# Layer scale on one core: the HBM layout in two blocks of 64 rows, and one head of 8 rows instead of two of 4

## The chip, the cores and the metric

The kernel runs on one core of one Trainium2 chip. The metric is device time in microseconds (us); the kernel before takes 119.68 us, the median of three runs (119.56 to 119.86). Of the core, this kernel uses VectorE (DVE) for the arithmetic, TensorE (PE) for one small product and to pass signals on, and the queues of SyncE (SP) and ScalarE (ACT) to issue transfers. The transfers of both queues are carried out by the same 16 DMA engines, in packets.

## The reference

```
B, S, D = 1024, 16, 512          # all bf16
def reference(x, y, gamma):      # x, y: [B, S, D]; gamma: [D]
    return x + gamma * y
```

Per call 16.78 MB of x and as much of y are read and 16.78 MB are written, 50.33 MB in all, for one multiplication and one addition per element.

## The kernel before, in words

The tensors are taken as 16384 rows of 512 elements (1 KB each), 128 rows to each of the 128 partitions of the on-chip memory (SBUF). The list BLOCKS (L7) cuts HBM into blocks: a block of n rows holds 128 n rows of the tensor, and partition p takes n that follow each other. So in the block of 64 rows each partition's data is one run of 64 KB, in that of 60 rows one of 60 KB, and in the first block one of 4 KB. A transfer of n rows then moves one packet of n KB for each partition, and each DMA engine serves 8 partitions.

All of y (128 KB per partition) has its place in y_sb, where the result also is formed. x_sb holds only 76 rows: the second part of x goes over rows of the first part that have been added. The fourth number of an x entry in the lists below is its row in x_sb.

The order of the work is written out by hand, in three lists:

- SP (L12 to L19): y 0 to 4, y 4 to 68, x 4 to 68, y 68 to 128, x 68 to 120, x 120 to 128.
- ACT (L20): x 0 to 4, gamma, then the stores 4 to 68, 0 to 4 and 68 to 128.
- DVE (L28): multiplications ("m") and additions ("a") over the PIECES of 8, 16, 44, 52 and 8 rows (L9). Multiplication is y_sb = y_sb * gamma_sb (L180), addition is y_sb = x_sb + y_sb (L189).

The function ring (L113) issues a list in its order. EARLY says how many of a list's first transfers are moved ahead of the program's opening barrier (L197 to L203). AHEAD says at which entry the queue waits for the signal s_held, which TensorE gives when the transfer HOLD, y 0 to 4, has landed (L147 to L149). So x 4 to 68 and what follows it on SP, and gamma on ACT, are issued only then. A load of x into rows of x_sb that were used waits for the additions of the pieces there (frees, L102). A store waits for the additions of its rows; the first store also waits for s_go, which TensorE gives when RELEASE, x 68 to 120, has landed (L157 to L159). DVE takes the same landing through s_rel.

gamma is one row; a product on TensorE with a column of ones spreads it over the partitions (L152) and DVE copies it to gamma_sb (L154). The multiplications need it. The program ends on SP's wait for all stores (L195).

Of the kernel before, what the change touches and what calls it, by code (L numbers as in the profile page):

```python
# [3 lines left out]

BLOCKS = [4, 64, 60]  # L7

PIECES = [8, 16, 44, 52, 8]  # L9


SP = [  # L12
    ('y', 0, 4),
    ('y', 4, 68),
    ('x', 4, 68, 4),
    ('y', 68, 128),
    ('x', 68, 120, 24),
    ('x', 120, 128, 0),
]  # L19
ACT = [('x', 0, 4, 0), ('g',), ('s', 4, 68), ('s', 0, 4), ('s', 68, 128)]  # L20

EARLY = (2, 1)

HOLD, AHEAD = ('y', 0, 4), (2, 1)

RELEASE = ('x', 68, 120, 24)

DVE = [('m', 0), ('m', 1), ('m', 2), ('a', 2), ('a', 0), ('a', 1), ('m', 3), ('m', 4), ('a', 3), ('a', 4)]  # L28
MULT, ADD = mybir.AluOpType.mult, mybir.AluOpType.add


def _take(sem, n, eng):


    return eng.wait_ge(sem, n).then_inc(sem, -n)  # L35


def kernel(
# [18 lines left out]
    rows = N // P  # L57
    n = len(PIECES)
    assert sum(PIECES) == rows
    starts = [sum(PIECES[:c]) for c in range(n + 1)]  # L60
    dt = xf.dtype
    edges = [sum(BLOCKS[:c]) for c in range(len(BLOCKS) + 1)]
    assert edges[-1] == rows

    def rows_of(t, a, b):

        c = max(c for c in range(len(BLOCKS)) if edges[c] <= a)
        assert b <= edges[c + 1]
# [6 lines left out]
    y_sb = nc.alloc_sbuf_tensor("y_sb", [P, rows, D], dt).ap()  # L75
    x_loads = [w for w in ACT + SP if w[0] == "x"]
    y_loads = [w for w in SP + ACT if w[0] == "y"]
    stores = [w for w in SP + ACT if w[0] == "s"]
    for loads in (x_loads, y_loads, stores):
# [9 lines left out]
    s_add, s_go, s_rel, s_end, s_out = sem("s_add"), sem("s_go"), sem("s_rel"), sem("s_end"), sem("s_out")  # L89
    added = [a for kind, *a in DVE if kind == "a"]  # L90
    order = {a[0]: k for k, a in enumerate(added)}

    def meets(a, b, c, d):
        return a < d and c < b
# [4 lines left out]
    def x_at(row):  # L99
        return next(w[3] + row - w[1] for w in x_loads if w[1] <= row < w[2])  # L100
# [12 lines left out]
    def ring(eng, what, n_early, n_ahead):  # L113

        known, went = 0, False
        for k, w in enumerate(what):
            kind = w[0]
            if k == n_ahead:
                _take(s_held[eng], 1, eng)
            need = frees(w) if kind == "x" else pieces_of(w[1], w[2]) + list(w[3:]) if kind == "s" else []  # L120
            need = max((order[c] + 1 for c in need), default=0)
            if kind == "s" and not went:
                _take(s_go, 1, eng)
                went = True
            if need > known:
                eng.wait_ge(s_add, need)
                known = need
            if kind == "g":
                i = eng.dma_start(out=gamma_row, in_=gamma.unsqueeze(0)).then_inc(s_gamma, 16)
            elif kind == "x":  # L130
                to = x_sb[:, w[3] : w[3] + w[2] - w[1], :]
                i = eng.dma_start(out=to, in_=rows_of(xf, w[1], w[2])).then_inc(s_load[w], 16)
            elif kind == "y":
                r = slice(w[1], w[2])
                i = eng.dma_start(out=y_sb[:, r, :], in_=rows_of(yf, w[1], w[2])).then_inc(s_load[w], 16)
            else:
                r = slice(w[1], w[2])
                i = eng.dma_start(out=rows_of(of, w[1], w[2]), in_=y_sb[:, r, :]).then_inc(s_out, 16)
            if k < n_early:
                early.append(i.ins)  # L140

    ring(nc.sync, SP, EARLY[0], AHEAD[0])
    ring(nc.scalar, ACT, EARLY[1], AHEAD[1])

# [11 lines left out]

    _take(s_load[RELEASE], 16, nc.tensor)  # L157
    nc.tensor.sem_inc(s_go, 1)
# [4 lines left out]
    def need(loads, c):  # L163
        for w in loads:
            if w not in landed and meets(starts[c], starts[c + 1], w[1], w[2]):
                if w == RELEASE:
                    _take(s_rel, 1, nc.vector)
                elif w == HOLD:
                    _take(s_held[nc.vector], 1, nc.vector)
                else:  # L170
                    _take(s_load[w], 16, nc.vector)
                landed.add(w)

    for kind, *args in DVE:
        c = args[0]
        yt = y_sb[:, starts[c] : starts[c + 1], :]
        if kind == "m":
            need(y_loads, c)
            g = gamma_sb[:, None, :].to_broadcast([P, PIECES[c], D])
            nc.vector.tensor_tensor(out=yt, in0=yt, in1=g, op=MULT).then_inc(s_dve, 1)  # L180
            open_mults += 1
        else:
# [4 lines left out]
            at = x_at(starts[c])  # L187
            xt = x_sb[:, at : at + PIECES[c], :]
            nc.vector.tensor_tensor(out=yt, in0=xt, in1=yt, op=ADD).then_inc(s_add, 1)  # L189
# [44 lines left out]
```

## Time and profile before

| What | us |
|---|---|
| Median of three runs | 119.68 (119.56 to 119.86) |
| Profiled execution: its span, which is the time that the profile gives for it | 118.2 |
| DVE busy | 70.1 (59% of the span) |
| PE busy | 0.6 |
| DMA, mean over the span | 426 GB/s |

The page of the profile lists busy time by engine, the DMA queues (q1 is SP's, q10 is ACT's) with the share of 16 engines' span that their packets took, and groups of instructions by line. The time of a DMA issue (SPq, ACTq) is only that of issuing; the transfer runs on after it. Windows cut the span at chosen moments and give, for each stretch, its duration, the busy time of the engine asked for with its number of instructions, the TensorE clock, the DMA engines' busy share and what they moved. A packet is counted where it starts, so the share of a short window can pass 1.

### The profile page before, as it was taken

How to read it: one execution, taken by the hardware profiler on the slowest of the kernel's cores; microseconds unless marked ns; L12 is line 12 of the kernel's file. 1: busy time of each engine (PE TensorE's matmuls, PEld its weight loads, DVE VectorE, ACT ScalarE, POOL GpSimd, SP SyncE). 2: the span in 40 equal slices, each digit the busy share in tenths (PEclk: the TensorE clock that was granted, in tenths of full speed). 3: DMA queues.
4: the chain of work that ended last, by engine and by line, in shares of the span. 5: the costliest groups of instructions: out<-in, count | busy, mean ns of one | idle time of the engine just before them, and what ended most of it. 6: DMA issues, size and time to landing. Idle time of an engine off the chain costs nothing. (4 is left out here: it accounts for less than half of the span.)

```text
span 118.2 us, 91 instructions
## 1 busy us (share of the span) xinstructions
PE 0.6 (0%) x1; PEld 0.1 (0%) x1; DVE 70.1 (59%) x12; POOL 0.2 (0%) x4
## 2 busy tenths in 40 slices
PE   0000100000000000000000000000000000000000
PEld 0000000000000000000000000000000000000000
DVE  0000200089999969999999999999999900000000
POOL 0000000000000000000000000000000000000000
DMA  6999889988899879879969696898899889799793
GB/s 248 461 666 399 355 355 399 665 355 355 355 599 466 355 333 624 374 333 499 499 288 576 288 576 288 360 637 355 355 576 488 355 355 510 333 582 416 333 499 166
DMA packets 1442, 50.33 MB, mean 426 GB/s; under 512 B 161, under 2 KB 162, under 8 KB 546
## 3 DMA queue, kind: packets, MB, share of 16 engines
q1 hardware_dynamic: 864, 33.03, 64.8%
q10 hardware_dynamic: 578, 17.30, 33.9%
HBM read 33.56 MB, written 16.78 MB: 426 GB/s over the span
## 5 line engine op out<-in xcount | busy, mean ns | idle before, releaser
L180 DVE TENSOR_TENSOR y_sb<-y_sb,gamma_sb 128x4096 bf16<-128x4096 bf16 (+3 forms) x5 | 34.7, 6981 | 10.9 <-DVEq L35 10.9
L189 DVE TENSOR_TENSOR y_sb<-x_sb,y_sb 128x4096 bf16<-128x4096 bf16 (+3 forms) x5 | 34.7, 6981 | 1.2 <-DVEq L35 1.1
L154 DVE CAST gamma_sb<-gamma_ps 128x512 bf16<-128x512 f32 x1 | 0.7, 692 | 10.2 <-DVEq L35 10.2
L146 DVE MEMSET ones_row<- 1x128 bf16 x1 | 0.2, 165 | 2.0 <-PEq L51 2.0
L152 PE MATMUL gamma_ps<-gamma_row,ones_row 1*128 1x512 bf16 x1 | 0.6, 581 | 11.6 <-PEq L35 11.6
L152 PEld LDWEIGHTS gamma_ps<-gamma_row,ones_row 1*128 1x128 bf16 x1 | 0.1, 101 | 11.6 <-issue 11.6
L218 POOL MEMSET const-bfloat16-1.0<- 128x1 bf16 x1 | 0.1, 101 | 0.0
L218 POOL MEMSET const-uint8-127<- 128x1 uint8 x1 | 0.1, 101 | 0.0
L218 POOL MEMSET const-float32-0.0<- 128x1 f32 x1 | 0.1, 98 | 0.2 <-issue 0.2
L218 POOL MEMSET const-float32-1.0<- 128x1 f32 x1 | 0.1, 98 | 0.0
## 6 DMA issues: line engine op xcount, KB each, us to landing
y_sb<-in_y_dram SPq DMA_DIRECT2D x1, 7680.0 KB, 57.3
out_dram<-y_sb ACTq DMA_DIRECT2D x1, 7680.0 KB, 23.8
x_sb<-in_x_dram SPq DMA_DIRECT2D x1, 6656.0 KB, 21.7
x_sb<-in_x_dram SPq DMA_DIRECT2D x1, 1024.0 KB, 22.0
y_sb<-in_y_dram SPq DMA_DIRECT2D x1, 512.0 KB, 3.4
x_sb<-in_x_dram ACTq DMA_DIRECT2D x1, 512.0 KB, 4.2
out_dram<-y_sb ACTq DMA_DIRECT2D x1, 512.0 KB, 22.3
y_sb<-in_y_dram SPq DMA_DIRECT2D x1, 23.4
```

Of the source, the lines that this page charges most:

```text
L146: nc.vector.memset(ones_row, 1.0).then_inc(s_ones, 1)
L152: nc.tensor.matmul(gamma_ps, ones_row, gamma_row, start=True, stop=True).then_inc(s_ps, 1)
L154: nc.vector.tensor_copy(out=gamma_sb, in_=gamma_ps).then_inc(s_dve, 1)
L180: nc.vector.tensor_tensor(out=yt, in0=yt, in1=g, op=MULT).then_inc(s_dve, 1)
L189: nc.vector.tensor_tensor(out=yt, in0=xt, in1=yt, op=ADD).then_inc(s_add, 1)
L218: nc = _bacc.Bacc("TRN2", target_bir_lowering=False, num_devices=1)
```

## The change

HBM is cut into two blocks of 64 rows, so each partition's data lies in two runs of 64 KB. The two heads of 4 rows (y on SP, x on ACT) become one head, the first 8 rows of y on SP; those are rows of the block, 8 KB for each partition out of its 64. Behind it SP loads y 8 to 64, x 0 to 64, y 64 to 128, x 64 to 120 and x 120 to 128. ACT has no load ahead of the barrier and issues gamma and two stores of 64 rows, where it had three stores. HOLD and RELEASE name the transfers that now stand in these places. The pieces are 20, 44, 56 and 8 rows, in eight DVE instructions instead of ten. x_sb keeps 76 rows (20 + 56).

```
-BLOCKS = [4, 64, 60]
-PIECES = [8, 16, 44, 52, 8]
+BLOCKS = [64, 64]
+PIECES = [20, 44, 56, 8]
 SP = [
-    ('y', 0, 4),
-    ('y', 4, 68),
-    ('x', 4, 68, 4),
-    ('y', 68, 128),
-    ('x', 68, 120, 24),
+    ('y', 0, 8),
+    ('y', 8, 64),
+    ('x', 0, 64, 0),
+    ('y', 64, 128),
+    ('x', 64, 120, 20),
     ('x', 120, 128, 0),
 ]
-ACT = [('x', 0, 4, 0), ('g',), ('s', 4, 68), ('s', 0, 4), ('s', 68, 128)]
-EARLY = (2, 1)
-HOLD, AHEAD = ('y', 0, 4), (2, 1)
-RELEASE = ('x', 68, 120, 24)
-DVE = [('m', 0), ('m', 1), ('m', 2), ('a', 2), ('a', 0), ('a', 1), ('m', 3), ('m', 4), ('a', 3), ('a', 4)]
+ACT = [('g',), ('s', 0, 64), ('s', 64, 128)]
+EARLY = (2, 0)
+HOLD, AHEAD = ('y', 0, 8), (2, 0)
+RELEASE = ('x', 64, 120, 20)
+DVE = [('m', 0), ('m', 1), ('a', 1), ('a', 0), ('m', 2), ('m', 3), ('a', 2), ('a', 3)]
```

## The prediction

> **What bounds the kernel now.** I read the page's head and its DMA parts first, then the windows cut where the packet size changes, then the timeline around the hand-overs, then the groups by shape.
>
> ```profile
> span 118.2 us, 91 instructions
> PE 0.6 (0%) x1; PEld 0.1 (0%) x1; DVE 70.1 (59%) x12; POOL 0.2 (0%) x4
> ...
> q1 hardware_dynamic: 864, 33.03, 64.8%
> q10 hardware_dynamic: 578, 17.30, 33.9%
> ```
>
> The two DMA queues together keep the 16 DMA engines busy for 64.8 + 33.9 = 98.7% of the span; VectorE (DVE) has 59%. The chain of waits ends in the second store as 12.53 us of "issue" between two adds, which tells nothing here: the bound is the DMA engines. The windows say how well each stretch of them runs (duration, DVE busy, clock, DMA share, GB/s):
>
> ```profile
> 1.00:3.65 2.65, 0.17 (x1) 1.00 0.98 385
> 3.65:42.36 38.71, 19.11 (x4) 1.00 1.01 434
> 42.36:60.51 18.15, 17.07 (x4) 1.00 1.00 433
> 60.51:76.26 15.75, 15.75 (x3) 1.00 1.00 433
> 76.26:78.75 2.49, 2.34 (x2) 1.00 1.09 464
> 78.70:98.03 19.33, 15.69 (x2) 1.00 1.01 437
> 98.03:99.28 1.25, 0.00 (x0) 1.00 0.92 377
> 99.28:117.80 18.52, 0.00 (x0) 1.00 0.99 428
> ```
>
> In order these are: both 4-row heads (4 KB packets); y and x of rows 4 to 68 (64 KB packets); y 68 to 128 (60 KB); x 68 to 120 (52 KB); x 120 to 128 (8 KB); store 4 to 68; store 0 to 4 (4 KB); store 68 to 128. A packet is counted at its start, so a window's edge can borrow bytes: the fifth window's 464 holds first packets of the store, and by its own bytes x 120 to 128 is 1.049 MB / 2.49 us = 421 GB/s. No stretch after 3.65 waits for anything: each begins where the last ends, at 433 to 434 GB/s. All that can be won lies in the head (385) and the short store (377); all that can be lost is a hole between two transfers. How near the holes are, the timeline shows:
>
> ```profile
> 0.00 0.85 SPq L135 DMA_DIRECT2D y_sb<-in_y_dram  x2
> 0.13 0.38 ACTq L132 DMA_DIRECT2D x_sb<-in_x_dram  x1
> ...
> 3.90 0.50 ACTq L129 DMA_DIRECT2D gamma_row<-in_gamma_dram  x1
> ...
> 12.32 0.69 DVE L154 CAST gamma_sb<-gamma_ps 128x512 bf16<-128x512 f32 x1 [10.16 <-DVEq L35]
> ...
> 55.37 2.53 SPq L132 DMA_DIRECT2D x_sb<-in_x_dram  x2
> 61.80 16.22 DVE L180 TENSOR_TENSOR y_sb<-y_sb,gamma_sb 128x26624 bf16<-128x26624 bf16 x2
> 77.41 17.36 ACTq L138 DMA_DIRECT2D out_dram<-y_sb  x3
> 78.17 16.23 DVE L189 TENSOR_TENSOR y_sb<-x_sb,y_sb 128x26624 bf16<-128x26624 bf16 x2
> ```
>
> The first packet comes 1.00 us after the first issue. The last adds end at 78.17 + 16.23 = 94.40, the second large store is issued at 94.43 (the page's last DMA row has 23.8 us from there to landing, which is the span's end), and its packets begin at 99.28 only because the queue is full until then: 4.9 us to spare.
>
> **The change part by part.** The bytes stay 50.33 MB, so I sum stretches of DMA time from 1.00 on.
>
> *Head.* Two 4-row transfers on two queues (8 + 8 packets of 4 KB per engine) become one of 8 rows on SP's queue (8 packets of 8 KB per engine), the same 1.049 MB; ACT loses its early issue. Nearest rows: the old head, 2.65 us, and x 120 to 128, the same bytes in 8 KB packets, 2.49 us. The head also has the start-up of the first packets, so I take 2.55, between the two: -0.10 us, bounds -0.16 and 0. One bound more: whether y's next 56 rows stand ready when the head ends at 3.55. SP issues both loads back to back within 0.85 us, as now (the second from about 0.4); now that second load's packets begin at 3.65, after ACT's transfer was served in between. With that transfer gone I put the gap at nothing; if 3.65 were fixed, the head step gives 0.
>
> *The wait on the head.* x 0 to 64, y 64 to 128 and gamma are issued when the head has landed. Now the head lands at 3.4 and SP issues x at 3.71; a y head of 8 rows lands some 0.7 later, so SP issues at about 4.4 and ACT issues gamma at about 4.7. Behind SP's wait stand x and y; they are covered by y 8 to 64, in the queue until 20.5. gamma now takes from 3.90 to 11.5 to land and the cast ends at 13.0; 0.8 later is 13.8, and the first multiply cannot start before y's 64 rows are in, about 21.8. Cost nothing, with 8 us of cover.
>
> *Loads.* At 433.5 GB/s: y 8 to 64, 7.34 MB, 16.93 us, to 20.48; x 0 to 64, 8.39 MB, 19.35, to 39.83; y 64 to 128 19.35, to 59.18; x 64 to 120 16.93, to 76.11; x 120 to 128 2.49, to 78.60. Between head and first store that is 75.05 us for the bytes that took 75.10 (3.65 to 78.75). So this step is 0 but for rounding, unless DVE is late with a buffer.
>
> *DVE, does it hold an issue?* Elements stay the same in 8 instructions instead of 10. From the groups by shape, 26624 elements take 14.02 us and 22528 take 11.89, so 0.521 ns each: 28672 takes 15.09, 10240 some 5.5. Now the large y wait ends at 61.80, 1.29 after its stretch; the like gives 21.8 for the first multiplies (5.5 + 11.9, to 39.2) and 41.0 for the add of 44 rows, to 52.9. That add frees rows 20 to 64 of x_sb, and SP issues x 64 to 120 at 52.9, needed at 59.18: 6 us to spare (now 55.37 for 60.51). The add of 20 rows ends at 58.4 and frees x 120 to 128, needed at 76.11. The second half's multiplies run 60.5 to 77.7, the adds 77.9 to 95.2.
>
> *Stores.* The first waits, as now, for x 64 to 120 landing and is issued some 1.3 us before x 120 to 128 runs out (now 77.41, packets by 78.73): hidden under the same 8 rows. 2 x 8.39 MB replace 8.39 + 0.52 + 7.86. The short store's 1.25 us becomes 1.21 at 434: -0.04, and I take -0.05 with one boundary less; bounds -0.08 and 0. The second is issued at 95.2, three quarters of a us later, and is needed at 78.60 + 19.3 = 97.9, not at 99.28: the spare falls from 4.9 to 2.7 us. An issue takes 1.0 us (first packet of all) to 1.32 (77.41 to 78.73) to give packets, so still nothing.
>
> *Two rules weighed.* The block of rows 4 to 68 is laid out 64 KB apart per partition and runs at 434; the 60 KB block at 433; so both halves at 64 KB cost nothing by the rows. The Trainium skill, "DMA: Bandwidth & Descriptors", section "Latency and other measured facts", speaks against it: HBM rows at large powers of two run slower, 207 GB/s at a pitch of 512 KiB, in copies between HBM tensors, against 214 padded; it has no figure for 64 KiB. An estimate by that page's 3% on the 23.6 MB that change pitch would be +1.8 us. [...]
>
> *Sum.* -0.10 + 0 - 0.05 = -0.15 us: span 118.2 to 118.05. The profiled execution's own time is given as its span; the median of the runs, 119.68, is 1.48 above it and I carry that over: 119.53, say 119.55.
>
> **The rivals.** *The queue runs dry at the start* (slower). y 8 to 64 now has only the head before it on its queue. If its packets came only once the head has landed, as the 3.65 after the landing at 3.4 would also allow, they begin near 4.2 + 1.0 = 5.2 instead of 3.55: +1.65, less 0.15, span 119.7, time 121.2. It decides once packets start after 4.0. Against it: later loads on that queue follow each other before the earlier one's landing (x 4 to 68, issued at 3.71, took 39.5 us by the DMA rows and so landed at 43.2; the next packets came at 42.36).
>
> *The second store comes late* (slower). If an issue takes over 2.7 us to give packets, a hole opens at 97.9. The longest seen is 0.42 to 3.65 = 3.2, for a load that stood behind others; that gives a hole of 0.5 and 120.0. For it: the spare is the only one that the change nearly halves. Against it: that load's packets had others to wait for, and this store follows on its own queue.
>
> *The pitch or the 8 KB pieces read 64 KB apart run slower.* Against it the 434 above; half a per cent on 23.6 MB, the most that windows of 433 and 434 leave open, is +0.27, with the gain 119.8, inside what counts as the same.
>
> *All gains at their ends.* 8 KB head at the 421 of its row and no start-up, short store gone, -0.24, plus 0.1 to 0.2 if engines start more evenly: 119.2 to 119.4.
>
> **How the numbers follow.** A difference below 0.3% (0.36 us, 119.32 to 120.04) is about what a measurement of this kernel cannot tell from none; the three runs spread by 0.30. Chances: forecast 0.68, dry queue 0.10, late store 0.08, slower reads 0.06, all gains 0.08. Faster by over 0.3%: half of the last, and 0.08 of the forecast through scatter, 0.12. Slower: the dry queue, half of the late store, 0.02 each of slower reads and scatter, 0.18. Same: the rest, 0.70. The range 119.25 to 120.1 takes in the forecast with both bounds and the scatter, the late store at 0.5 and the slower reads, and leaves out the dry queue.
>
> **What would show it.** Right: the windows of after are 8 KB head to about 3.55, no DMA share below 0.95 up to 117.6, first large store issued near 77.3, second near 95.2, span 117.9 to 118.2. The head step is wrong if the second load starts after 3.7; the cover is gone if the DMA row shows empty slices after 97.9; the pitch is wrong if a 64 KB stretch is below 430 GB/s. The prediction is wrong if any hole over 0.4 us stands between two transfers, or if the span stays and the time around it moves.

## The result, and the profile after

The changed kernel took 120.11 us (median of 13 runs, 119.65 to 120.62) beside 119.73 us of the kernel before (13 runs, 119.56 to 119.94): a ratio of 1.0029, 95% interval 1.0018 to 1.0041. The forecast was 119.55 with a range to 120.1, so the time lies 0.01 outside the upper end, and the kernel got slower by 0.38 us where a gain of 0.13 was forecast. The runs of the changed kernel also lie two and a half times as far apart as those of the kernel before (0.97 us against 0.38). The profiled execution took 120.21 us, with a span of 118.9.

The page's head, DMA queues and last part, of the kernel after:

```profile
span 118.9 us, 86 instructions
PE 0.6 (0%) x1; PEld 0.1 (0%) x1; DVE 70.0 (59%) x10; POOL 0.2 (0%) x4
...
q1 hardware_dynamic: 864, 33.55, 66.1%
q10 hardware_dynamic: 290, 16.78, 32.6%
```

The DMA engines are still busy for 98.7% of the span, and the packets of ACT's queue fell from 578 to 290 (the x head and the short store are gone from it). Yet the span is 0.7 us longer: busy engines, moving less per us. The windows, cut where one transfer follows the other (duration, DVE busy, clock, DMA share, GB/s), of the kernel after:

```profile
0.98:3.67 2.69, 0.17 (x1) 1.00 0.99 375
3.67:20.67 17.00, 0.69 (x1) 1.00 1.01 434
20.67:40.09 19.42, 17.29 (x2) 1.00 1.00 432
40.09:59.71 19.62, 17.29 (x2) 1.00 1.00 428
59.71:76.90 17.19, 16.23 (x2) 1.00 1.00 427
76.90:79.41 2.51, 2.09 (x2) 1.00 0.97 411
79.41:98.73 19.32, 16.27 (x2) 1.00 1.00 435
98.73:118.50 19.77, 0.00 (x0) 1.00 0.98 424
```

They are the head, y 8 to 64, x 0 to 64, y 64 to 128, x 64 to 120, x 120 to 128 and the two stores. Each transfer begins where the last ends: no hole anywhere. The loads took 75.74 us (3.67 to 79.41) where before they took 75.07 (3.65 to 78.72), and 0.53 of the 0.67 lies in y 64 to 128 (19.62 against a forecast 19.35) and x 64 to 120 (17.19 against 16.93). The first store runs at 435 GB/s, and the packets of the second follow each other as closely (the last window also holds the end, where no new packet starts).

Inside those two loads the loss is not spread evenly. Each engine moves eight packets of a load, one after the other, so a load is eight waves of 16 packets that start within about half a us. Windows of single waves, the fourth to the sixth of y 64 to 128 and then of x 64 to 120:

```profile
47.34:49.76 2.42, 2.42 (x1) 1.00 1.00 433
49.76:52.41 2.65, 2.65 (x1) 1.00 0.99 396
52.41:54.85 2.44, 2.44 (x2) 1.00 1.00 430
66.05:68.19 2.14, 2.14 (x1) 1.00 0.99 429
68.19:70.50 2.31, 2.31 (x1) 1.00 1.01 397
70.50:72.64 2.14, 2.14 (x1) 1.00 1.00 429
```

One wave of each load, the fifth, took 0.2 us too long (2.65 against 2.42; 2.31 against 2.14). In the packet records all 16 packets of these waves lose, 0.11 to 0.27 us each. I call this a long wave, and give for a wave the mean excess of its 16 packets over their size at 27.08 GB/s, the rate of one engine in undisturbed packets (65,536 bytes in 2.42 us). The waves of the head and the first wave behind it belong to the start of the stream (up to 0.09 us in the latter) and are not counted.

The timeline after shows that the covers held:

```profile
4.98 0.53 ACTq L129 DMA_DIRECT2D gamma_row<-in_gamma_dram  x1
...
13.54 0.69 DVE L154 CAST gamma_sb<-gamma_ps 128x512 bf16<-128x512 f32 x1 [11.39 <-DVEq L35]
21.60 17.29 DVE L180 TENSOR_TENSOR y_sb<-y_sb,gamma_sb 128x10240 bf16<-128x10240 bf16 x2 [7.37 <-DVEq L35]
...
53.08 5.73 SPq L132 DMA_DIRECT2D x_sb<-in_x_dram  x2
60.67 17.29 DVE L180 TENSOR_TENSOR y_sb<-y_sb,gamma_sb 128x28672 bf16<-128x28672 bf16 x2 [2.22 <-DVEq L35]
78.10 17.95 ACTq L138 DMA_DIRECT2D out_dram<-y_sb  x2
```

gamma is spread at 14.2, 7 us before the first multiplication; x 64 to 120 is issued at 53.1 and needed at 59.7; the second store is issued near 95.7 (78.10 + 17.95 less the issue itself) and its packets follow at 98.73 without a gap.

### The profile page after: what moved, and what is told of

Its sections match the earlier page's. It is cut to its first block, busy times and chain, and to the rows that moved or that the text cites. A ratio compares the mean times of both kernels' runs of the same rounds, so it can differ in the third digit from the quotient of the medians.

```text
span 118.9 us, 86 instructions
## 1 busy us (share of the span) xinstructions
PE 0.6 (0%) x1; PEld 0.1 (0%) x1; DVE 70.0 (59%) x10; POOL 0.2 (0%) x4
## 5 line engine op out<-in xcount | busy, mean ns | idle before, releaser
L180 DVE TENSOR_TENSOR y_sb<-y_sb,gamma_sb 128x10240 bf16<-128x10240 bf16 (+3 forms) x4 | 34.6, 8688 | 9.6 <-DVEq L35 9.6
L189 DVE TENSOR_TENSOR y_sb<-x_sb,y_sb 128x22528 bf16<-128x22528 bf16 (+3 forms) x4 | 34.6, 8688 | 2.7 <-DVEq L35 2.7
```

## The experiments

What was expected of each run speaks of theories. *Layout* means that reads of the second block lose time because of where its 64 KB pieces lie (later called *address*) or how far apart (later *pitch*); *head* that the loss is the start-up of the 8-row head; *outside* that something not in this core slows reads now and then; *DVE* that VectorE's work on SBUF holds up the writes of loads. Where blocks or heads change, the pieces and the order of DVE's work follow them; the cuts of code leave that out.

**The changed kernel, three times more**, on three different chips, no edit. The first:

> The changed kernel once more, for a second profile. Layout theory (reads of the second 64 KB block lose time because of where it lies): again packets of the fourth and later waves in y 64 to 128 and x 64 to 120 take some 0.2 us too long, 0.3 to 0.6 us in all, span 118.6 to 119.2. Head theory (the loss is the 8 KB head's start-up): the second load starts 2.7 us after the first packet again, and the rest runs at 433 GB/s or more, span about 118.4. Outside theory (something not in this core slows reads now and then): the long packets stand in other places or are gone, span anywhere from 118.2 to 119.3.

119.78 us (10 runs, 119.57 to 120.00), before 119.80: ratio 0.9997 [0.9986, 1.0008]. The wave at 49.9 was long again, by 0.19 us, the one near 68 was not; span 118.6. So the place recurs, but the 0.3% of the first measurement did not.

> The changed kernel once more beside the others. Pitch theory: the wave at 49.8 (fourth of y 64 to 128) is 0.2 us long a third time; runs from 119.6 to 120.0 or up to 120.6. Outside theory: no long wave at that place. Head: second load from 3.67 to 3.9.

119.80 us (12 runs, 119.59 to 120.54), before 119.81: 1.0008 [0.9993, 1.0024]. This profile had no long wave of 0.05 us or more. Its windows are what the forecast had meant, but for the head:

```profile
1.01:3.80 2.79, 0.17 (x1) 1.00 1.05 391
3.80:20.76 16.96, 0.69 (x1) 1.00 1.00 430
20.76:40.11 19.35, 17.29 (x2) 1.00 1.00 434
40.11:59.58 19.47, 17.30 (x2) 1.00 1.00 431
59.58:76.50 16.92, 16.02 (x2) 1.00 1.00 434
```

> The changed kernel beside the next three. So far three profiles of it lost 0.66, 0.37 and 0.22 us to long read packets behind the head, the kernel before 0.15 and 0.50. Address theory: where a wave is long, it is the fourth or a later one of y 64 to 128 or x 64 to 120. Outside theory: other places too. Runs 119.6 to 120.6.

119.87 us (12 runs, 119.54 to 120.14), before 119.81: 1.0000 [0.9991, 1.0010]. The wave at 68.1 was long, by 0.17 us. Over all four sets, 12 of 47 runs of the changed kernel are above 120.1 us and 2 of 103 of the kernel before; seven of the twelve are in the first set.

**The kernel before, profiled again** (no edit):

> The kernel before once more, for a second profile on the chip that the others here run on. If a strided head starts slower than a contiguous one: the first 64 KB packets at 3.65 to 3.75 again, no wave of long packets. If the start varies by itself: the first 64 KB packets anywhere up to 4.1.

119.82 us against 119.81, ratio 1.0003 [0.9993, 1.0013]. The profiled execution was the longest of its eight, 120.06 us. Its windows (head; y and x of rows 4 to 68; y 68 to 128; x 68 to 120):

```profile
1.01:3.66 2.65, 0.17 (x1) 1.00 1.00 377
3.66:42.46 38.80, 19.03 (x4) 1.00 1.00 434
42.46:60.76 18.30, 17.25 (x4) 1.00 1.00 430
60.76:76.68 15.92, 15.92 (x3) 1.00 1.00 428
```

So the kernel before has the same losses in a longer execution: 18.30 against 18.15 and 15.92 against 15.75, with long waves near 56 (0.07), 58 (0.10) and 68.6 us (0.13), and these in a block whose pieces are 60 KB apart. A distance of 64 KB is not needed for them. The rows at 433 and 434 on which the forecast stood belong to one undisturbed execution, and in all likelihood to the fastest of the three: in the 13 profiles of 118 to 119 us whose execution's time is on record, that time is 1.32 to 1.33 us above the span, and 118.23 + 1.33 is 119.56.

**Heads of before, second block of 64 rows:**

```
-BLOCKS = [64, 64]
+BLOCKS = [4, 60, 64]
-SP:  y 0 8, y 8 64, x 0 64, ...       ACT: g, s 0 64, s 64 128
+SP:  y 0 4, y 4 64, x 4 64, ...       ACT: x 0 4, g, s 4 64, s 0 4, s 64 128
```

> The two 4-row heads of before, then a block of 60 rows and one of 64 (y 4 to 64, x 4 to 64, y 64 to 128, x 64 to 120, x 120 to 128). Layout theory: slower than before by 0.3 to 0.5 us, with long packets in the second half's loads. Head theory: equal to before within 0.1 us. Outside theory: equal on the median, with long packets in no fixed place.

119.77 us (12 runs, 119.69 to 120.10), ratio 0.9998 [0.9989, 1.0008]; no long wave, though y 64 to 128 and x 64 to 120 lie at the same addresses within their tensors as in the change. The layout theory in its simple form falls as far as 12 runs and one profile go: a second block of 64 rows at this place did not bring the loss.

**Layout of the change, two heads of 4 rows out of the 64-row block:**

```
 BLOCKS = [64, 64]
-SP:  y 0 8, y 8 64, x 0 64, ...       ACT: g, s 0 64, s 64 128
+SP:  y 0 4, y 4 64, x 4 64, ...       ACT: x 0 4, g, s 0 64, s 64 128
```

> The layout of the change (two blocks of 64 rows, two stores of 64 rows) with two 4-row heads on two queues as before. Layout theory: as slow as the change, +0.3 to +0.5 us against before. Head theory: equal to before, or 0.05 us faster by the short store that is gone. Outside theory: between the two, with a wide spread.

120.51 us (6 runs, 120.44 to 120.65), 1.0058 [1.0042, 1.0074]: slower than any theory had it, and steadily so. Head, y 4 to 64, x 4 to 64 and y 64 to 128:

```profile
1.00:4.06 3.06, 0.17 (x1) 1.00 0.94 312
4.06:22.59 18.53, 0.69 (x1) 1.00 1.01 430
22.59:40.74 18.15, 17.02 (x3) 1.00 1.00 433
40.74:60.06 19.32, 17.70 (x4) 1.00 1.00 434
```

The head took 3.06 us, 0.4 more than the two contiguous ones of before, and y 4 to 64 lost 0.38, with long waves at 8.6 (0.12) and 11.1 us (0.16). VectorE had next to nothing to do then (0.69 us in that window); the second half lost nothing. Why these two heads start more slowly was not looked into further.

**Head and first block of the change, second half as 60 and 4 rows:**

```
-BLOCKS = [64, 64]
+BLOCKS = [64, 60, 4]      # y 64 124, y 124 128, x 64 120, x 120 124, x 124 128; stores 64, 60, 4
```

> The head and first block of the change, but the second half as a block of 60 rows and one of 4 (y 64 to 124, y 124 to 128, x 64 to 120, 120 to 124, 124 to 128, stores 64, 60 and 4 rows). The 4-row transfers cost 0.05 us each by the rows of before, 0.15 in all. Layout theory: the loss in the second half goes, +0.1 to +0.2 us against before for head and short transfers. Head theory: +0.3 to +0.5. Outside theory: as the change, with a wide spread.

119.93 us (12 runs, 119.75 to 120.17), 1.0013 [1.0003, 1.0023], no long wave in the profile. It is the number that the layout theory gave, but after the two runs above it can't be read as proof of it.

**An 8-row head as a block of its own:**

```
-BLOCKS = [64, 64]
+BLOCKS = [8, 60, 60]      # y 0 8, y 8 68, x 0 8, x 8 68, y 68 128, ...; stores 60, 8, 60
```

> One head of 8 rows of y, as in the change, but as a block of its own, so that it lies in one contiguous piece of 1 MB; then y 8 to 68, x 0 to 8, x 8 to 68, and the second half in a block of 60 rows; stores of 60, 8 and 60 rows. If the slow head of the change comes from its rows being 64 KB apart: first packets near 0.35 us instead of 0.45 to 0.51, second load from 3.6, span 118.1 to 118.3, time -0.1 to +0.05 us against before. If it comes from the 8 KB size or from having one queue: second load from 3.8 to 3.9, +0.1 to +0.3. Pitch theory: no wave of long packets, since no block is of 64 rows; outside theory: some.

120.00 us (10 runs, 119.97 to 120.35), 1.0020 [1.0011, 1.0029]. The contiguous head is not faster but slower, 3.03 us to the second load's first packet, and its first 32 packets took 0.52 us on the mean (0.45 to 0.50 in the four profiles of the change). That the change's head is slow because its rows are 64 KB apart falls.

**A pitch of 62 KB:**

```
-BLOCKS = [64, 64]
+BLOCKS = [62, 62, 4]      # y 0 8, y 8 62, x 0 62, y 62 124, y 124 128, x 62 116, x 116 124, x 124 128
```

> The change with a pitch of 62 KB instead of 64 KB: head y 0 to 8 out of a block of 62 rows, then y 8 to 62, x 0 to 62, y 62 to 124, y 124 to 128, x 62 to 116, x 116 to 124, x 124 to 128, stores 62, 62 and 4. The three 4-row transfers cost 0.05 us each. Pitch theory: no wave of 16 packets with a mean excess over 0.1 us, runs within 0.4 us of each other; with the slow head +0.1 to +0.3 us against before. Outside theory: waves with 0.2 us excess and runs up to 1 us apart, as the change had. If the head is slow only at a power-of-two distance, its first packets are near 0.35 us and the total is +0.05.

120.37 us (5 runs, 120.24 to 120.49), 1.0048 [1.0036, 1.0060]. No long wave in the loads of 54 and 62 rows and runs close together, as the pitch theory wanted, but 0.56 us slower where 0.1 to 0.3 was expected: the short transfers cost far more than 0.05 each (the last 4-row store took 2.1 us from its first packet at 116.6 to the end of its last at 118.8, for 0.5 MB). The head took 2.93 us: a pitch off the power of two does not help it either.

**VectorE on the first row of each piece alone**, so that the other rows are stored as loaded:

```
-yt = y_sb[:, starts[c] : starts[c + 1], :]
+yt = y_sb[:, starts[c] : starts[c] + 1, :]
```

> The change with VectorE on the first row of each piece alone (the other rows are stored as loaded, so most of the arithmetic is left out). The transfers stay. DVE theory (VectorE's reads and writes hold up what the DMA engines write to SBUF): no long wave in any load behind the head, all runs within 0.25 us, 119.5 to 119.7. Address and outside theories: as wide as the changed kernel itself, up to 120.3 or more.

119.84 us, 12 runs from 119.67 to 120.42: as wide as the changed kernel beside it (119.54 to 120.14), where the DVE theory wanted all within 0.25. It falls by that spread; the profiled execution (119.74) had no long wave.

**No head:**

```
-SP:  y 0 8, y 8 64, x 0 64, ...       EARLY = (2, 0)
+SP:  y 0 64, x 0 64, ...              EARLY = (2, 1), HOLD = y 0 64
```

> The layout of the change without a head: y 0 to 64 as the first transfer, x 0 to 64 right behind it, gamma ahead of the barrier on ACT's queue. Head theory (the small packets at the start cost 0.3 to 0.5 us against their bytes at 433 GB/s): the first transfer ends at 1.1 + 19.4 + 0.2 = 20.7 or earlier and the store phase starts 0.2 to 0.4 us before the changed kernel's, 119.3 to 119.5 when no wave is long. If the start costs the same whatever the packets' size: 119.6 to 119.8.

120.04 us (9 runs, 119.89 to 120.36), 1.0024 [1.0015, 1.0033]. Its first loads:

```profile
1.00:20.91 19.91, 0.17 (x1) 1.00 1.00 418
20.91:40.25 19.34, 16.37 (x3) 1.00 1.00 434
40.25:59.59 19.34, 18.90 (x3) 1.00 1.00 434
59.59:76.52 16.93, 15.74 (x2) 1.00 1.00 434
```

The first load takes 19.91 us, 0.57 more than the next of the same size. So a start with 64 KB packets costs no less than one with small ones; small packets are not to blame. Behind it this layout reads at 434.

**The two blocks swapped in HBM:**

```
+h = len(BLOCKS) - 1 - c
-block = t[P * edges[c] : P * edges[c + 1]]...
+block = t[P * edges[h] : P * edges[h + 1]]...
```

> The change with its two HBM blocks in the other order: rows 0 to 64 of each partition lie in the upper block, rows 64 to 128 in the lower; times, sizes and places in SBUF stay. Address theory: the second half's loads lose no wave; if anything is long, it is the fourth waves of y 8 to 64 or x 0 to 64 (near 12 and 30 us). Place-in-time theory: the waves near 50 and 68 us are long as before.

119.90 us (12 runs, 119.61 to 120.59), 1.0014 [0.9999, 1.0028]. As wide as the change; the profiled execution was the shortest of the twelve and had no long wave, so where the long waves of its longer runs lie is not known. Inconclusive on the place.

**Reads alone.** To see more waves in one profile, all arithmetic was left out and one half was read over and over, each buffer waiting for its last landing while the other buffer's load filled the queue; then y was stored as loaded:

```
for k in range(TIMES):                 # 6, or 14 in the longer ones
    _take(...)                         # y of the round before has landed
    load(nc.sync, ('y', 64, 128), s_y)
    _take(...)                         # x of the round before has landed
    load(nc.sync, ('x', 64, 120, 20), s_x)
```

> Reads alone, for statistics: the change's head, y 8 to 64 and x 0 to 64, then y 64 to 128 and x 64 to 120 six times over, then the two stores; the arithmetic is left out and y is stored as loaded. 96 waves of the second block in one profile, about 297 us. Address theory (long waves come from where the 64 KB block lies): several waves over 0.1 us mean excess, at the same place in each repetition. Outside theory: long waves in no fixed place, and as many in the other three kernels. If they need VectorE or the waits of the real kernel: none.

> The same with the second half in a block of 60 rows and one of 4 (y 64 to 124 and x 64 to 120 six times). Address and pitch theory: no wave over 0.1 us, and executions within 0.3 us of each other around 291 us. Outside theory: as many long waves as at 64 KB.

> The same with the lower block read six times over (y 0 to 64, x 0 to 56) and y 64 to 128 once at the end, about 317 us. If it is the upper block's addresses: no long wave in the repetitions. If it is the pitch of 64 KB: as many as in the upper block. Outside theory: as many in every kernel.

> The upper 64 KB block six times over, but behind the two contiguous 4-row heads and a first block of 60 rows. Address theory: long waves at the same places as behind the 8-row head. If how the head spreads the engines in time decides it: none, or at other places.

Of the 12 repeated loads in each profile, counting waves with a mean excess of 0.05 us or more:

| Kernel | time, us | long waves (of 96) | excess of the 12 loads, us |
|---|---|---|---|
| upper block, 64 KB | 300.94 | 5 | 0.73 |
| upper block, 60 KB | 294.51 | 0 | 0.15 |
| lower block, 64 KB | 320.11 | 3 | 0.62 |
| upper block, 64 KB, contiguous heads | 300.99 | 3 | 0.41 |

The first three kernels took 3 to 4 us more than expected, and the four runs at 60 KB lay 0.52 us apart, where under 0.3 was expected (0.26, 0.50 and 0.59 in the kernels at 64 KB). The long waves need neither VectorE nor the upper block. They were not at the same place in each repetition; but eight of the eleven were the fifth wave of their load. The Trainium skill, "DMA: Bandwidth & Descriptors", section "The descriptor swizzle", has each engine serve two groups of four neighbouring partitions, 32 apart, by which, if it takes them in that order, the fifth wave is where every engine jumps to another place in HBM; the packet records here carry no address, so no run shows it. The 60 KB kernel had none, which favoured the distance of 64 KB. Against it stands the last kernel of the table: its first block, read once before the repetitions, has pieces 60 KB apart, and there a wave of y 4 to 64 was long by 0.07 us (near 17.5) and one of x 4 to 64 by 0.13 (near 31.3). Its x load, beside the 18.15 of an undisturbed load of 60 rows:

```profile
22.12:40.50 18.38, 1.00 1.00 428
```

The last pair was to tell the distance from chance:

> Reads alone again, the upper half of the change's layout fourteen times over (y 64 to 128 and x 64 to 120, 28 loads of 8 waves), about 591 us. Pitch theory: as in the shorter runs at 64 KB, about a quarter of the loads have a wave of 0.05 us or more mean excess, nearly always the fifth of the eight (where each engine goes on to its second group of partitions), 0.05 us a load on the mean. Outside theory: as many in the kernel at 62 KB.

> The same with blocks of 62, 62 and 4 rows (y 62 to 124 and x 62 to 118 fourteen times), about 585 us, at a pitch that is neither 64 KB nor the 60 KB tried before. Pitch theory: no wave of 0.05 us or more in 28 loads, 0.01 us a load on the mean. If only 60 KB is free of them, or chance was: as at 64 KB.

591.31 and 583.17 us. Of 28 loads each, 64 KB had three long waves (0.05, 0.15 and 0.10 us) and 62 KB one (0.07); excess 0.82 and 0.61 us, 0.03 and 0.02 a load. A quarter of the loads against none was expected, so this pair does not carry the pitch theory. Nor did the place hold: the three were the first wave of their load and the one the third, none the fifth, so the jump between groups of partitions is not borne out as the cause. What the pair shows instead is when the losses occur. The same load of y, 64 KB, at six times of the longer run (no DVE there):

```profile
40.16:59.50 19.34, 1.00 0.99 427
76.51:96.03 19.52, 1.00 1.00 430
149.30:168.81 19.51, 1.00 1.00 430
221.95:241.27 19.32, 1.00 1.00 434
367.10:386.45 19.35, 1.00 1.00 434
512.27:531.62 19.35, 1.00 1.00 434
```

After 170 us the loads take 19.32 to 19.35 us, without a long wave to the end of the repetitions at 548. In all six profiles of reads alone the last long wave of the repetitions, where there is one, is over by 216 us; four of them end their repetitions by 259 us, so the quiet after it rests on the two longer ones. An end of this kind speaks against a cause outside the core, unless that too begins with the program. It looks like something in how the 16 streams stand to each other, which each loss shifts a little until they no longer hinder one another; that is argued, not shown.

## Why the prediction was wrong, point by point

**What bounds the kernel: right.** DMA engines busy 98.7% before and after, no hole behind the head.

**The head, -0.10: wrong in size and sign.** The term was 2.55 us from the first packet to the second load's first. In eleven profiles with the change's head (the change, its variants and the reads alone) it is 2.69 to 2.92. Before it was 2.65 in both profiles; the same two heads in front of a 60-row block took 2.92 and 2.93. The mistake was to take the steady row of 8 KB packets (2.49, from the end of the loads) and to add only 0.06 for the start. The first 16 packets of 8 KB took 0.56 to 0.69 us in the change's four profiles, against 0.31 in the steady row, and a start with 64 KB packets, without a head, costs 0.57 us of its own. Against the 2.65 of before the head step is worth +0.04 to +0.27 in place of -0.10. Its sign, a second load after 3.7, is absent in the first profile (3.67) and there in the other three (3.78 to 3.91). Why the same two heads take 0.27 more in front of a 60-row block is not shown.

**The wait on the head, gamma, DVE's holds on issues, the covers: right.** x was issued at 4.78 (forecast 4.4), the first multiplication ran at 21.60 (21.8), x 64 to 120 was issued at 53.08 (52.9), the second store near 95.7 (95.2) with 3.0 us to spare (2.7).

**Stores, -0.05: not contradicted, too small to see.** From the first store's first packet to the end of the span it is 39.50 and 39.57 us in the two profiles of before and 39.35 to 39.55 in the four of after.

**Loads, "0 but for rounding": this step failed.** It held the loads of both kernels to the 433 and 434 GB/s of one execution. The terms, from packet to packet (the head to the second load's first packet, the loads to the first store's, the stores to the end of the span):

| Profile | head, us | loads, us | stores, us | span, us |
|---|---|---|---|---|
| Forecast | 2.55 | 75.05 | -0.05 against before | 118.05 |
| Before | 2.65 | 75.07 | 39.50 | 118.2 |
| Before, again | 2.65 | 75.50 | 39.57 | 118.7 |
| After | 2.69 | 75.74 | 39.46 | 118.9 |
| After, again | 2.88 | 75.41 | 39.35 | 118.6 |
| After, third | 2.77 | 75.18 | 39.48 | 118.4 |
| After, fourth | 2.91 | 75.36 | 39.55 | 118.8 |

The forecast's 75.05 is the undisturbed floor. In the first set the loads were worth +0.67 us where the sum had 0, and the head +0.04 where it had -0.10; with the stores 0.04 shorter that makes the 0.65 by which the span grew. The loads of the change lost 0.1 to 0.7 us over the floor, in long waves and lesser ones, and so did one of the two executions of before (0.4). Long executions are more frequent with the change (12 of 47 against 2 of 103 above 120.1 us; 5 of 34 against 2 of 90 without the first set).

**Carrying 1.48 us from span to time: a mixture.** The time is 1.32 to 1.33 us above the span of the same execution. The 1.48 took the median of three runs and the span of what was in all likelihood the fastest, so it holds some 0.15 of ordinary loss, unnamed, while the term for the loads was set at nothing.

**The rivals.** Neither the dry queue nor the late store happened. Of the third, slower reads, the outcome came in the first set, but not shown is its cause, the distance of 64 KB or the 8 KB pieces. Its price of +0.27, called the most that the windows leave open, was read from the same single execution, and the loads then lost 0.67. Its sign, a 64 KB stretch below 430 GB/s, did come (428 and 427), but the 60 KB block of the kernel before shows 430 and 428 in its second profile, so the sign does not tell the layouts apart. The rule on power-of-two distances that was weighed there is neither borne out nor refuted at 64 KB: undisturbed loads run at 434, the last pair did not separate 64 from 62 KB, and nothing near the +1.8 us estimated there was seen.

**The size of the result.** The +0.29% belongs to one set of runs; three others give 0.9997, 1.0008 and 1.0000, all with intervals that hold no change. The forecast of no difference that can be told fits those, and their medians (119.78 to 119.87) lie inside the range. That is in part luck: head and loads were off there too, and the kernel before loses as much in its ordinary runs (medians of 119.80 and 119.81). The forecast 119.55 is near the floor that the changed kernel reaches in its best runs (119.54 to 119.65), no lower than that of before (119.56 to 119.69). What stays open: what a long wave comes from, why the first set had more long executions than the other three, and what in the change makes them more frequent. The 64 KB distance is a candidate for the frequency alone (14 long waves in 64 repeated loads against 1 in 40 at 60 and 62 KB, but from four and two profiles, and long waves stand in blocks at 60 KB too).

## What to carry to other kernels

When one profile shows a DMA-bound kernel at its ceiling, its rows are a floor: take a second profile before costing loads at nothing, since a few tenths of a us in the reads were larger than all the terms of this sum. Price a first transfer by a first transfer and not by a like-sized one in the middle of the stream. A difference of 0.3% between two kernels of which one has more than twice the spread needs more than one set of runs.

## What was not expected of the hardware

- Reads can lose 0.1 to 0.2 us in a whole wave, in all 16 of its packets, with the engines busy by the profile all the time; no store of before or after lost such a wave (436 and 435 GB/s in the first stores of the two).
- In repeated reads this had ended by itself by 216 us in every profile, and did not come back up to 548 us in the longer ones.
- The start of the stream costs 0.2 to 0.6 us against its bytes at full rate, with 4, 8 or 64 KB packets, contiguous or not.
